# Attention and gated FFN on one Trainium2 core: the last scores of batch 3 moved to the end of group 1, and the steady pattern begun one group earlier

## The chip, the cores and the metric

The kernel runs on one core of one Trainium2 chip. The metric is the device time of one execution in microseconds. The profile's span is about 1.8 us shorter than the time of the same run. A single-core run has no second die to be compared with; all runs that are used here were counted as undisturbed ("fast"). In the profile, PE is the matmul engine (TensorE), PEld its loading of weights, ACT is ScalarE, DVE is VectorE, POOL is Pool (GpSimd), and SPq is the DMA queue of SP; L281 is line 281 of the kernel. "Issue" is time in which an engine waited for nothing that the profile shows.

## The reference

```python
# attention: 8 batches, 8 heads, 576 positions, head size 64; window of 128, ALiBi slopes
scores = scale * q @ k.T
scores = where((rel >= 0) & (rel < 128), scores - slope * abs(rel), -1e9)
attn   = exp(scores - max); attn /= attn.sum() + 1e-9
x      = (attn @ v) -> 4608 tokens x 512
# FFN: 512 -> 1536 -> 512
out = (gelu(x @ w_gate) * (x @ w_val)) @ w_out
```

## The kernel before

The FFN goes over the tokens in nine groups of 512. Group g first computes 12 blocks (gate and value), then 8 half pieces of the output. The attention of later batches (576 tokens each) is woven into it: the scores of batch g+2 stand between the output pieces of group g. Then come a batch's row sums and reciprocals (parts 0 and 1 of the tokens), the spreading of the reciprocals over the partitions, and the product with v. Group 3 needs batch 3's values.

Reciprocals are spread in one of two ways. Batches 0 to 3 use matmuls. From batch 4 on it is done by DMA: one small transfer to DRAM (`rd`) and two that read it back, broadcast (`rb`). K and q of batches 2 and up are turned by DMA transposes. All these go through one queue, that of SP, in program order.

```python
    def transposes_dma(b):                       # L156: key first, then query
        for src, dst in ((ks, kT), (qs, qT)):
            nc.sync.dma_start_transpose(out=dst[b % 2]..., in_=src[b % 2]...)
    ...
    def sums(b, s):                              # L221: 24 matmuls with ones
        ps = bank()                              # one of 8 PSUM banks, in rotation
        ...
        nc.vector.reciprocal(sumrow[b][:, lo:hi], ps[:, 0:hi - lo])          # L230

    def spread_dma(b):
        d = d_pool.tile([4, 2, S], FP32, name="rd")
        nc.sync.dma_start(out=d..., in_=sumrow[b][0:128:16, :])              # L234
        for i in (0, 1):
            nc.sync.dma_start(out=recip[b][64 * i:64 * i + 64, :, :], ...)   # L236

    def spread_pe(b, s):                         # L244: fp32 matmuls, then copies (L251)
        ...
    def values(b, s, cs):                        # L262 matmuls with v, L268 product
        ...
    def gate_val(g, f):                          # L281, two banks; gelu L285, product L286
        ...
    def out_half(g, u):                          # L297, half of an output piece; osb L302
        ...
    todo = { 0: [...],
        1: [("s2", 2), ("s", 2, 0, (0, 1)), 0, ("s", 2, 0, (2, 3)), 1, 2,
            ("s", 2, 1, (0, 1), lambda: sums(2, 0)), 3, ("s", 2, 1, (2, 3)), ("s2", 3),
            ("spread", 2, 0), ("pv", 2, 0), 4, ("sum", 2, 1), ("s", 3, 0, (0, 1)), 5, 6,
            ("spread", 2, 1), ("pv", 2, 1), ("s", 3, 0, (2, 3)), 7],
        2: [("s", 3, 1, (0, 1), lambda: sums(3, 0)), 0, ("s", 3, 1, (2, 3)), 1,
            ("spread", 3, 0), ("pv", 3, 0), ("s2", 4), ("sum", 3, 1), 2,
            ("s", 4, 0, (0, 1)), 3, ("spread", 3, 1), ("pv", 3, 1), 4, ("s", 4, 0, (2, 3)), 5,
            ("s", 4, 1, (0, 1)), 6, 7, ("s", 4, 1, (2, 3))],
    }
    def steps(g):                                # the steady pattern, b = g + 2
        ...
        return [("s2", b), ("s", b, 0, (0, 1)), 0, 1, ("s", b, 0, (2, 3)), 2, 3,
                ("s", b, 1, (0, 1)), 4, 5, ("s", b, 1, (2, 3)), 6, 7]

    for g in range(NG):
        for b in ((), (2, 3), (4,))[g] if g < 3 else ():
            transposes_dma(b)                    # batch 4: at the start of group 2
        if g + 2 < B:
            load_v(g + 2)                        # Pool's queue; waits for values(g)
        for f in range(3 if g == 0 else 0, NF):
            gate_val(g, f)
            ...
            if 3 <= g < B - 1:
                if f == 0:
                    sums(g + 1, 0)
                    sums(g + 1, 1)
                    spread_dma(g + 1)
                    if g + 2 < B:
                        transposes_dma(g + 2)
                elif f in (8, 10):
                    for s in (0, 1):
                        values(g + 1, s, (f - 8, f - 7))
        if g + 3 < B:
            load_qk(g + 3)                       # Pool's queue; waits for transposes_dma(g + 1)
        for item in steps(g): ...
```

The softmax here doesn't subtract the row's maximum and nothing guards it: scores larger than these inputs give would overflow.

Of the kernel before, what the change touches and what calls it, by code (L numbers as in the profile page):

```python
# [26 lines left out]
def kernel(  # L27
# [11 lines left out]
    B, H, S, D = q.shape  # L39
# [23 lines left out]
    def bank():  # L63
        return psum.tile([128, 512], FP32, name="ps")
# [23 lines left out]
    def load_qk(b):  # L88
        load(qs[b % 2], q, b)
        load(ks[b % 2], k, b)  # L90
# [18 lines left out]
    def load_v(b):  # L109
        load(vb[b % 2], v, b)  # L110
# [28 lines left out]
    def transpose(b, what, c, copy):  # L139
        ps = bank().bitcast(BF16)  # L140
        for j in range(5):
            nc.tensor.transpose(  # L142
                out=ps[:, 128 * j:128 * j + 128],
                in_=(qs, ks)[what][b][:, j, 128 * c:128 * c + 128], identity=ident)
        copy(out=(qT, kT)[what][b][:, :, c, :],
             in_=ps[:, 0:640].rearrange("p (j t) -> p j t", t=128))
# [7 lines left out]
    def transposes_dma(b):  # L154
        for src, dst in ((ks, kT), (qs, qT)):
            nc.sync.dma_start_transpose(  # L156
                out=dst[b % 2].rearrange("p j c t -> p (j c) t"),
                in_=src[b % 2].rearrange("p j x -> p (j x)"))
# [49 lines left out]
    def prob(b, s, c, i, j, n):  # L208
        if (s, j) == (0, 2):
            return probs2[b][:, c, i, 0:n]  # L210
        return probs[b, s, c][:, i, PCOL[s][j]:PCOL[s][j] + n]
# [3 lines left out]
    def sums(b, s):  # L215

        ps = bank()
        for j, a, e in PIECES[s]:
            for i in (0, 1):
                for c in range(4):  # L220
                    nc.tensor.matmul(  # L221
                        out=ps[32 * c:32 * c + 32, a:e],
                        lhsT=ones[:, min(j, 1), i, :], rhs=prob(b, s, c, i, j, e - a),
                        start=(i == 0 and j == 2 * s), stop=(i == 1 and j == 2 * s + 2),
                        skip_group_check=True)
        if s == 0:
            sumrow[b] = r_pool.tile([128, S], FP32, name="r")
            recip[b] = r_pool.tile([128, 4, S], FP32, name="rb")
        lo, hi = PART[s]
# [4 lines that stand above are left out]
        nc.sync.dma_start(out=d.rearrange("c i s -> (c i) s"), in_=sumrow[b][0:128:16, :])  # L234
        for i in (0, 1):
            nc.sync.dma_start(  # L236
                out=recip[b][64 * i:64 * i + 64, :, :],
                in_=d[:, i, :].unsqueeze(0).to_broadcast((64, 4, S)))
# [14 lines left out]
    def values(b, s, cs):  # L253
        lo, hi = PART[s]
        pss = []
        for c in cs:
            ps = bank()
            pss.append(ps)
            for j, a, e in PIECES[s]:
                for i in (0, 1):  # L260
                    h = 2 * c + i
                    nc.tensor.matmul(  # L262
                        out=ps[64 * i:64 * i + 64, a:e],
                        lhsT=vb[b % 2][:, j, 64 * h:64 * h + 64],
                        rhs=prob(b, s, c, i, j, e - a),
                        start=(j == 2 * s), stop=(j == 2 * s + 2), skip_group_check=True)
        for c, ps in zip(cs, pss):
            nc.vector.tensor_tensor(  # L268
                out=xT[:, c, b * S + lo:b * S + hi], in0=ps[:, 0:hi - lo],
                in1=recip[b][:, c, lo:hi], op=ALU.mult)  # L270
# [3 lines left out]
    def gate_val(g, f, lo=0, hi=512):  # L274
        if g not in hid:
            hid[g] = h_pool.tile([128, NF, 512], BF16, name="hT")
        t0 = 512 * g
        pg, pv = bank(), bank()
        for w, ps in ((wg, pg), (wv, pv)):
            for c in range(4):  # L280
                nc.tensor.matmul(  # L281
                    out=ps[:, 0:hi - lo], lhsT=w[:, c, 128 * f:128 * (f + 1)],
                    rhs=xT[:, c, t0 + lo:t0 + hi], start=(c == 0), stop=(c == 3))
        gl = g_pool.tile([128, 512], BF16, name="gelu")
        nc.scalar.activation(out=gl[:, 0:hi - lo], in_=pg[:, 0:hi - lo], func=AF.Gelu)  # L285
        nc.vector.tensor_tensor(out=hid[g][:, f, lo:hi], in0=pv[:, 0:hi - lo],  # L286
                                in1=gl[:, 0:hi - lo], op=ALU.mult)
# [3 lines left out]
    def out_half(g, u):  # L291
        t, half = u // 2, u % 2
        if half == 0:
            acc[g] = bank()
        po = acc[g]
        for f in range(6 * half, 6 * half + 6):
            nc.tensor.matmul(  # L297
                out=po, lhsT=hid[g][:, f, 128 * t:128 * (t + 1)],
                rhs=wo[:, f, :], start=(f == 0), stop=(f == NF - 1))
        if half == 1:  # L300
            osb = o_pool.tile([128, DM], FP32, name="osb")
            nc.scalar.copy(out=osb, in_=po)  # L302
            r0 = 512 * g + 128 * t
            nc.sync.dma_start(out=out[r0:r0 + 128, :], in_=osb)
# [83 lines left out]
    for t in (qs[0], ks[0]):  # L388
# [11 lines left out]
        1: [("s2", 2), ("s", 2, 0, (0, 1)), 0, ("s", 2, 0, (2, 3)), 1, 2,  # L400
            ("s", 2, 1, (0, 1), lambda: sums(2, 0)), 3, ("s", 2, 1, (2, 3)), ("s2", 3),
            ("spread", 2, 0), ("pv", 2, 0), 4, ("sum", 2, 1), ("s", 3, 0, (0, 1)), 5, 6,
            ("spread", 2, 1), ("pv", 2, 1), ("s", 3, 0, (2, 3)), 7],
        2: [("s", 3, 1, (0, 1), lambda: sums(3, 0)), 0, ("s", 3, 1, (2, 3)), 1,
            ("spread", 3, 0), ("pv", 3, 0), ("s2", 4), ("sum", 3, 1), 2,
            ("s", 4, 0, (0, 1)), 3, ("spread", 3, 1), ("pv", 3, 1), 4, ("s", 4, 0, (2, 3)), 5,
            ("s", 4, 1, (0, 1)), 6, 7, ("s", 4, 1, (2, 3))],
    }

    def steps(g):  # L410
        b = g + 2
        if g in todo:
            return todo[g]
        if b >= B:
            return range(8)
        return [("s2", b), ("s", b, 0, (0, 1)), 0, 1, ("s", b, 0, (2, 3)), 2, 3,
                ("s", b, 1, (0, 1)), 4, 5, ("s", b, 1, (2, 3)), 6, 7]
# [2 lines left out]
           "pv": lambda b, s: values(b, s, range(4))}  # L420

    for g in range(NG):
        for b in ((), (2, 3), (4,))[g] if g < 3 else ():
            transposes_dma(b)
        if g + 2 < B:
            load_v(g + 2)
        for f in range(3 if g == 0 else 0, NF):
            gate_val(g, f)
            if g == 0 and f >= 8:
                for w in (0, 1):  # L430
                    transpose(1, w, f - 8, (act, dve)[w])
            if 3 <= g < B - 1:
                if f == 0:
                    sums(g + 1, 0)
                    sums(g + 1, 1)
                    spread_dma(g + 1)
                    if g + 2 < B:
# [5 lines that stand above are left out]
            load_qk(g + 3)  # L443
        for item in steps(g):
            if isinstance(item, int):
                out_half(g, item)
            else:
                RUN[item[0]](*item[1:])
# [30 lines left out]
```

## Time and profile before

| | before |
|---|---|
| time, median of 3 runs | 367.69 us (367.64 to 367.73) |
| span of the profiled run | 365.5 us |
| PE busy | 347.8 us, 95% |
| first FFN matmul of groups 2, 3 (PE's timeline) and 4, 5 (chain of waits) | 111.78, 151.99, 190.14, 227.54 us |
| a steady group (4 and later) | 37.40 us |

Where PE did not wait, the chain starts a block 0.08 to 0.16 us later than PE's timeline does (190.14 against 189.98).

The page gives each engine's busy share. The chain of waits gives, in order of time, the work that set the end: start, length, engine and line. A long unbroken run of PE pieces means that only PE's work counts there; a piece of another engine or of a DMA means that PE stood still for it. The timelines give each engine's instructions with the idle time before them and what ended it, in brackets. The lines are in the prediction below.

### The profile page before, as it was taken

To read this page: it belongs to the slowest core of one execution; us is meant where nothing else is said; L and a number is where in the kernel's file an instruction comes from. 1 tells how busy PE (TensorE), PEld (TensorE's weight loads), DVE (VectorE), ACT (ScalarE), POOL (GpSimd) and SP (SyncE) were. 2 spreads that over 40 slices of the span, in tenths; PEclk is the share of its full clock that TensorE was granted. 3 is DMA by queue.
4 is the path that set the end of the run, shared out by engine and by line. 5 is a ranking of instruction groups with operands and counts; after the bars stand their busy time and mean duration, and the time that the engine had idled before them with its cause. 6 is when DMAs were issued, how large, how long until landed. Compare 5 with 4: busy or idle time off the path is not lost.

```text
span 365.5 us, 6601 instructions
## 1 busy us (share of the span) xinstructions
PE 347.8 (95%) x2614; PEld 171.3 (47%) x2656; DVE 188.6 (52%) x306; ACT 187.3 (51%) x339; POOL 107.9 (30%) x140
## 2 busy tenths in 40 slices
PE   3799999999999999999999999999999999999995
PEld 2455545444454445444445444444444444444442
DVE  4794448543695469475547454655564404302320
ACT  5863487434966376943783368436842223323321
POOL 8945859913519202900850040000000000000000
PEclk9779999999999999999999999999999999999999
DMA  9999999999969994999991992094205020011002
GB/s 103 136 199 178 177 163 184 174 153 200 162 116 121 136 92 81 143 103 217 127 196 50 228 97 89 33 221 53 87 32 131 0 109 7 0 60 58 0 29 88
DMA packets 151168, 41.41 MB, mean 113 GB/s; under 512 B 138816, under 2 KB 144448, under 8 KB 151136
## 3 DMA queue, kind: packets, MB, share of 16 engines
q0 software_dynamic: 112608, 18.88, 67.8%
q1 hardware_dynamic: 38528, 22.10, 27.2%
q8 instruction: 21, 0.34, 0.4%
q14 instruction: 11, 0.09, 0.1%
HBM read 42.47 MB, written 9.51 MB: 142 GB/s over the span
## 4 chain that ended last, share of the span: by engine, by line
PE 86%; ACT 5%; DVE 3%; DMA 3%; issue 1%; POOL 1%; POOLq 0%; SPq 0%; ACTq 0%; DVEq 0%
PE ps L281 50%; PE ps L297 23%; PE ps L262 4%; ACT P L170 4%; PE ps L163 4%; DMA qT<-qs 3%; PE ps L221 2%; PE ps L244 2%; DVE r L230 1%; DVE P L173 1%; DVE xT L268 1%; ACT emask L346 1%; PE ps L142 1%; POOL ks L104 0%; ACT L170 0%
## 5 line engine op out<-in xcount | busy, mean ns | idle before, releaser
L286 DVE TENSOR_TENSOR hT<-ps,gelu 128x512 bf16<-128x512 f32 (+2 forms) x111 | 74.3, 674 | 121.9 <-PE ps L281 109.3
L285 ACT ACTIVATE gelu<-ps 128x512 bf16<-128x512 f32 (+2 forms) x111 | 64.9, 585 | 119.6 <-PE ps L281 117.2
L281 PE MATMUL ps<-xT,wg 128*128 128x512 bf16 (+2 forms) x430 | 110.6, 374 | 0.8
L281 PE MATMUL ps<-xT,wv 128*128 128x512 bf16 (+2 forms) x435 | 110.4, 373 | 0.6
L297 PE MATMUL ps<-wo,hT 128*128 128x512 bf16 x413 | 97.2, 380 | 1.5 <-issue 0.6
L170 ACT ACTIVATE P<-ps 128x512 bf16<-128x512 f32 x144 | 74.4, 632 | 7.1 <-PE ps L163 7.0
L281 PEld LDWEIGHTS <-wv 128*128 128x128 bf16 x444 | 43.3, 98 | 50.3 <-issue 0.2
L281 PEld LDWEIGHTS <-wg 128*128 128x128 bf16 x444 | 41.9, 98 | 48.9 <-issue 1.1
L173 DVE TENSOR_TENSOR P<-P,emask 128x1024 bf16<-128x1024 bf16 x72 | 48.3, 685 | 31.3 <-ACT P L170 31.0
L297 PEld LDWEIGHTS <-hT 128*128 128x128 bf16 x432 | 39.8, 98 | 49.0 <-issue 4.4
L84 POOL DMA_DIRECT2D vb<-in_v_dram x40 | 33.7, 862 | 75.8 <-PE ps L262 75.0
L302 ACT COPY osb<-ps 128x512 f32<-128x512 f32 x36 | 21.7, 603 | 37.2 <-PE ps L297 32.8
L84 POOL DMA_DIRECT2D qs<-in_q_dram x35 | 29.6, 877 | 24.9 <-DMA qT<-qs 12.9
L230 DVE RECIPROCAL r<-ps 128x320 f32<-128x320 f32 (+1 forms) x16 | 30.7, 1939 | 3.1 <-PE ps L221 3.1
L84 POOL DMA_DIRECT2D ks<-in_k_dram x35 | 29.6, 887 | 6.4 <-DMA qs<-in_q_dram 3.0
L163 PE MATMUL ps<-qT,kT 64*128 64x256 bf16 (+1 forms) x384 | 24.0, 254 | 3.0 <-DVE kT L136 1.3
L268 DVE TENSOR_TENSOR xT<-ps,rb 128x320 bf16<-128x320 f32 (+1 forms) x64 | 24.7, 449 | 0.8 <-DMA rb<-rd 0.8
L163 PEld LDWEIGHTS <-kT 64*128 64x128 bf16 x384 | 13.1, 96 | 16.9 <-issue 11.6
L262 PE MATMUL ps<-P,vb 128*64 128x128 bf16 (+2 forms) x384 | 19.4, 251 | 0.1
L262 PEld LDWEIGHTS <-vb 128*64 128x64 bf16 x384 | 15.4, 113 | 7.3 <-issue 7.2
L221 PE MATMUL ps<-P,ones 128*32 128x128 bf16 (+2 forms) x384 | 11.6, 256 | 1.3 <-DVE P L173 1.3
L221 PEld LDWEIGHTS <-ones 128*32 128x32 bf16 x384 | 8.5, 101 | 5.6 <-issue 4.5
(47 smaller groups left out, 91.3 us busy)
## 6 DMA issues: line engine op xcount, KB each, us to landing
out_dram<-osb SPq DMA_DIRECT2D x36, 256.0 KB, 2.7
rb<-rd SPq DMA_DIRECT2D x8, 576.0 KB, 7.1
vb<-in_v_dram POOLq DMA_DIRECT2D x32, 128.0 KB, 4.7
qs<-in_q_dram POOLq DMA_DIRECT2D x28, 128.0 KB, 6.7
ks<-in_k_dram POOLq DMA_DIRECT2D x28, 128.0 KB, 6.4
wg<-in_moe_w_gate_dram POOLq DMA_DIRECT2D x4, 384.0 KB, 11.0
wv<-in_moe_w_val_dram POOLq DMA_DIRECT2D x4, 384.0 KB, 12.2
wo<-in_moe_w_out_dram POOLq DMA_DIRECT2D x2, 768.0 KB, 10.9
```

Of the source, the lines that this page charges most:

```text
L84: nc.gpsimd.dma_start(out=t[lo:128, j, :].rearrange("p (h d) -> p h d", h=H), in_=src[b][:, 128 * j - 64 + lo:128 * j + 64, :].rearrange(" ...
L163: nc.tensor.matmul(out=ps[:, col:col + 128 * n].rearrange("p (n t) -> p n t", n=n), lhsT=blocks(kT, b, i, c, j, 1).rearrange("p n t -> p ( ...
L170: nc.scalar.activation(out=dst, in_=src, func=AF.Exp, scale=0.125)
L173: nc.vector.tensor_tensor(out=dst, in0=dst, in1=m, op=ALU.mult)
L221: nc.tensor.matmul(out=ps[32 * c:32 * c + 32, a:e], lhsT=ones[:, min(j, 1), i, :], rhs=prob(b, s, c, i, j, e - a), start=(i == 0 and j == ...
L230: nc.vector.reciprocal(sumrow[b][:, lo:hi], ps[:, 0:hi - lo])
L262: nc.tensor.matmul(out=ps[64 * i:64 * i + 64, a:e], lhsT=vb[b % 2][:, j, 64 * h:64 * h + 64], rhs=prob(b, s, c, i, j, e - a), start=(j == ...
L268: nc.vector.tensor_tensor(out=xT[:, c, b * S + lo:b * S + hi], in0=ps[:, 0:hi - lo], in1=recip[b][:, c, lo:hi], op=ALU.mult)
L281: nc.tensor.matmul(out=ps[:, 0:hi - lo], lhsT=w[:, c, 128 * f:128 * (f + 1)], rhs=xT[:, c, t0 + lo:t0 + hi], start=(c == 0), stop=(c == 3))
L285: nc.scalar.activation(out=gl[:, 0:hi - lo], in_=pg[:, 0:hi - lo], func=AF.Gelu)
L286: nc.vector.tensor_tensor(out=hid[g][:, f, lo:hi], in0=pv[:, 0:hi - lo], in1=gl[:, 0:hi - lo], op=ALU.mult)
L297: nc.tensor.matmul(out=po, lhsT=hid[g][:, f, 128 * t:128 * (t + 1)], rhs=wo[:, f, :], start=(f == 0), stop=(f == NF - 1))
```

## The change

The intent is to have the steady pattern from group 2 on. Batch 3's last score calls move from group 2 to the end of group 1; its sums move into group 2's FFN blocks; its reciprocals are spread by DMA in place of matmuls; and batch 4's transposes follow them in SP's queue, where they used to stand at the start of group 2. In group 2 alone the sums of part two come at `f == 2`, two blocks later than in the other groups.

```diff
             ("spread", 2, 0), ("pv", 2, 0), 4, ("sum", 2, 1), ("s", 3, 0, (0, 1)), 5, 6,
-            ("spread", 2, 1), ("pv", 2, 1), ("s", 3, 0, (2, 3)), 7],
-        2: [("s", 3, 1, (0, 1), lambda: sums(3, 0)), 0, ("s", 3, 1, (2, 3)), 1,
-            ("spread", 3, 0), ("pv", 3, 0), ("s2", 4), ("sum", 3, 1), 2,
-            ("s", 4, 0, (0, 1)), 3, ("spread", 3, 1), ("pv", 3, 1), 4, ("s", 4, 0, (2, 3)), 5,
-            ("s", 4, 1, (0, 1)), 6, 7, ("s", 4, 1, (2, 3))],
+            ("spread", 2, 1), ("pv", 2, 1), ("s", 3, 0, (2, 3)), 7, ("s", 3, 1, (0, 1)),
+            ("s", 3, 1, (2, 3))],
     }
@@
-        for b in ((), (2, 3), (4,))[g] if g < 3 else ():
+        for b in ((), (2, 3))[g] if g < 2 else ():
             transposes_dma(b)
@@
-            if 3 <= g < B - 1:
+            if 2 <= g < B - 1:
                 if f == 0:
                     sums(g + 1, 0)
+                if f == (2 if g == 2 else 0):
                     sums(g + 1, 1)
                     spread_dma(g + 1)
                     if g + 2 < B:
```

## The prediction

> **What bounds the kernel now.** I read the page's first two parts, then the chain of waits, then the timelines of PE, ScalarE, VectorE and the DMA-issuing queue around the groups that the diff touches.
>
> ```profile
> PE 347.8 (95%) x2614; PEld 171.3 (47%) x2656; DVE 188.6 (52%) x306; ACT 187.3 (51%) x339; POOL 107.9 (30%) x140
> ...
> PE   3799999999999999999999999999999999999995
> ```
>
> The reader is to see that PE is busy in every slice after the start, while the next busiest engines stand at half. So the time changes only if PE gets less work, or a gap opens or closes on PE. The chain of waits (start, length, what) gives PE's clock by group, since each group of 512 tokens begins with a stretch of L281 matmuls:
>
> ```profile
> 137.17 0.75 PE ps L244 x8
> ...
> 143.26 0.66 PE ps L244 x8
> ...
> 151.51 0.56 PE ps L163 x12
> 152.07 2.08 ACT P L170 x4
> 154.18 0.70 DVE P L173
> 154.93 0.60 PE ps L221 x21
> ...
> 190.14 1.73 PE ps L281 x8
> ...
> 227.54 1.73 PE ps L281 x8
> ...
> 264.94 1.73 PE ps L281 x8
> ```
>
> Groups 4 and 5 begin at 190.14 and 227.54, group 6 at 264.94: a steady group takes 37.40 us. The timeline of PE has group 2's first FFN matmul at 111.78 and group 3's at 151.99. So group 2 takes 40.21 us and group 3 takes 38.15, both more than steady. In group 2 the two L244 pieces are the spreading of the reciprocals by matmuls. At 152 to 155 the chain leaves PE: the sums wait for the last exponentials and mask.
>
> The steady pattern has almost no slack in one place, which the DMA queue's timeline shows (start, length of the issue, what):
>
> ```profile
> 160.48 0.71 SPq L234 DMA_DIRECT2D rd<-r  x1
> 162.36 1.35 SPq L236 DMA_DIRECT2D rb<-rd  x2
> 163.94 7.12 SPq L156 DMA_TRANSPOSE kT<-ks  x1
> 171.23 3.09 SPq L156 DMA_TRANSPOSE qT<-qs  x1
> ...
> 197.15 0.62 SPq L234 DMA_DIRECT2D rd<-r  x1
> 198.96 1.27 SPq L236 DMA_DIRECT2D rb<-rd  x2
> 200.45 6.58 SPq L156 DMA_TRANSPOSE kT<-ks  x1
> 207.20 3.08 SPq L156 DMA_TRANSPOSE qT<-qs  x1
> ```
>
> In a steady group four transfers hang behind the second reciprocal, in order. The second reciprocal ends at 160.46 and at 197.12 (VectorE's timeline: 156.70 + 3.76, 193.36 + 3.76). The query transpose, whose issue-to-landing row says 4.9 us in both windows, lands at 176.1 and 212.1. That is **15.0 to 15.7 us after the second reciprocal**. The scores that need it start at 176.88 and 214.35. So the slack was 0.7 and 2.2 us.
>
> **What the Trainium skill says.** "Perfetto Trace Analysis", Optimization Strategy: look for the gaps of the engine one optimizes for and for what releases them. That is the method here; the trace agrees that PE is that engine (95% busy). "PSUM — Partial Sum Buffer", PSUM: the matmul accumulator: eight banks, and they are PE's only way out. All eight serve this kernel in rotation, so a matmul group waits for the reader of the bank eight allocations back. "ScalarE: Activation LUTs", What ACT_TABLE_LOAD costs: a load takes about 1283 ns; the trace has 1.28 us for each. "DMA: Bandwidth & Descriptors", Issuing engines are not separate DMA queues: transfers of all issuing engines interleave on the same 16 engines. The trace agrees: a query transpose lands in 4.9 us when alone, and in 9.2 us where Pool's loads run beside it (issued at 88.54, with loads from 87.99).
>
> **The change part by part.**
>
> (a) *Removed: spreading batch 3 by matmuls.* 16 fp32 matmuls, 0.75 + 0.66 = 1.41 us of PE on the path. Four ScalarE copies (about 0.42 us each) and four VectorE copies (about 0.44) go too, off the path.
>
> (b) *Moved: the two score calls of batch 3 part two, from group 2 to the end of group 1.* PE work is the same: 24 matmuls, 0.55 us per 12, so 1.1 us. Group 1 grows by it and group 2 shrinks by it.
>
> (c) *Group 2 ends in the steady way*, with two output pieces behind the last scores. Group 3 then should be a steady group: 38.15 - 37.40 = 0.75 us gained.
>
> (d) *A new gap at the end of group 1.* Eight exponentials now stand behind the osb copy of piece 7 (start 112.25). ScalarE starts one every 0.5 us (eight took 4.03 us at 133.74). They start at 112.73 and the first ends near 113.35. PE finishes the scores near 113.0; the bank of the next FFN block is the one that this first exponential reads. So FFN block 0 starts at about **113.45** in place of 111.78: 1.1 us is the moved work, 0.57 is wait.
>
> (e) *After that no bank should be late.* Exponentials end at 116.8, the table load at 118.1, gelu 0 at 118.7, its product at 119.4. PE runs block 0 (1.73), sums (0.55), blocks 1 and 2, sums of part two, and wants block 3 at 119.75; its banks are free at 118.7 and 119.4. Block 4's first bank was read by the first reciprocal, over at 119.4 + 2.1 = 121.5, just when PE gets there. Placing the second sums behind block 2 and not block 0 makes this fit: the last mask ends near 117.5 and the second sums come at 119.2.
>
> (f) *The price: the DMA chain starts late.* VectorE's order in the changed program is product 0, reciprocal, products 1 and 2, reciprocal. The second one ends at about 121.4 + 1.3 + 1.7 = **124.4**, which is 10.9 us after block 0's start; in steady groups it is 7.0 (197.12 - 190.14) to 8.5. Behind it come rd (124.4), rb (126.3), key transpose (127.8) and query transpose (134.5). With the measured 15.0 to 15.7 it lands at 139.4 to 140.1 if alone. But Pool's loads of v for batch 5 are freed by the values of batch 3, which now end near 136, so they start while it runs. I add 0.5 to 1 us, chosen between nothing and the 4.3 us of the 9.2 us case, because only the last half overlaps. So it lands at **140.6**. PE without waiting would be at the scores of batch 4 at 113.45 + 24.2 (the steady 214.35 - 190.14) = 137.65. **PE waits 3.0 us there.** Batch 4's transposes used to be issued at 113.46, with no reciprocal ahead of them.
>
> (g) *rb lands near 134 to 135*, 9.7 to 10.5 us after the reciprocal as in the groups 3 and 4, while PE runs the first values at 130.2. VectorE sits still for some 3 us; PE feels it only at the second values (134.7), through banks, by at most half a microsecond, which is inside the wait of (f).
>
> **Sum.** From group 2's first block to group 4's, before: 190.14 - 111.78 = 78.36. After: 1.67 of (d), two steady groups 74.80, and the wait W of (f): 76.47 + W. That is a gain of 1.89 - W (the 1.41 and 0.75 of (a) and (c), some 0.3 of small issue gaps, less the new 0.57). With W = 3.0 the kernel loses 1.1 us: 367.69 + 1.1 = **368.8 us**. Nothing behind group 4 changes.
>
> **The rivals.** *A pure gain*: the query transpose comes in time, W near 0, 365.8 us. For it: (a) is certain, and the 2.2 us of slack in group 4 shows that the chain can be early. Against: the second reciprocal is some 4 us later in its group, more than that slack. *A larger loss*: Pool's loads slow the query transpose to its 9.2 us; it lands at 144, W is 6, 371.8 us. For it: that happened twice in the first groups. Against: those had loads beside them from their first moment, here only in the second half. *ScalarE becomes the bound at the seam*: if gelu 0 waits for more than I think, blocks 3 and 4 lose 1 to 2 us, but the chain of (f) moves with the reciprocals too, so the total rises by about the same amount: 370. For it: the banks of block 3 and 4 are free only just in time; against: ScalarE's durations there are well known.
>
> **Range and chances.** The terms (a) to (d) are known to 0.3 us; W is 1.4 to 4.7. So 367.2 to 370.4 holds it 8 times in 10, with 368.8 as the middle. The 2% line is 7.35 us away on either side; faster by that is not in the PE work removed, and slower needs a stall twice the worst one above: 0.01, 0.97, 0.02.
>
> **What would show each step.** (a): L244 with 48 matmuls in place of 64. (d): FFN of group 2 at 113.3 to 113.6 and ScalarE's table load ending near 118.1. (e): no PE gap over 0.3 us in blocks 0 to 8 of group 2. (f): the query transpose issued near 134.5, landing near 140.6, PE idle about 3 us before the s2 scores of batch 4, released by qT. (g): VectorE waiting about 3 us for rb. (c): groups 3 and 4 each 37.40. The prediction is wrong if qT lands before 138, if blocks 3 to 6 stall, or if group 3 loses its steady length to later loads.

## The result

The changed kernel took 372.94 us (median of 6 runs, 371.24 to 375.73), the kernel before beside it 367.72 (6 runs, 367.64 to 367.99). The ratio is 1.0146, 95% interval 1.0106 to 1.0186. Ratios here are the mean time of one kernel's fast runs over the mean of the other's from the same rounds, so not quite the ratio of the medians. By the 2% rule this is "same"; in truth the kernel is slower by about 5 us, and in these rounds its runs scatter over 4.5 us where those of the kernel before scatter over 0.35. The predicted 368.8 and its range up to 370.4 were too low.

The profiled run is the fastest of the six (371.24, span 369.5); the other five have no profile. First its page, the busy times and the row of PE over 40 slices:

```profile
PE 348.0 (94%) x2599; PEld 171.4 (46%) x2640; DVE 187.1 (51%) x302; ACT 186.1 (50%) x335; POOL 108.0 (29%) x140
...
PE   3899999999999995999999999999999999999995
```

PE's busy time did not fall although 1.4 us of matmuls went (the slower clock below is part of the answer), and a slice near 140 us, which used to be full, is half empty. The chain of waits shows the place (start, length, what):

```profile
111.69 0.78 PE ps L163 x18
112.47 0.66 ACT P L170
...
113.17 1.89 PE ps L281 x8
...
134.85 7.29 DMA qT<-qs
142.14 0.14 issue
142.28 1.47 PE ps L163 x16
...
156.87 1.73 PE ps L281 x8
...
194.27 1.73 PE ps L281 x8
```

Group 2 begins at 113.17 and group 3 at 156.87, so group 2 takes 43.70 us, 6.3 more than a steady group. Group 3 takes 194.27 - 156.87 = 37.40, as hoped. So the whole loss lies in group 2. Below, "the seam" is the place in group 2 where PE passes from the FFN blocks to the scores of batch 4 and the output pieces. The chain leaves PE for the query transpose of batch 4. PE's own timeline gives the wait in front of the first scores of batch 4, and Pool's and VectorE's timelines show what else went on:

```profile
142.28 1.47 PE L163 MATMUL ps<-qT,kT 64*128 64x128 bf16 x16 [4.43 <-DMA qT<-qs]
```

```profile
135.71 4.19 POOL L84 DMA_DIRECT2D vb<-in_v_dram  x5 [14.85 <-PE ps L262]
142.68 4.19 POOL L84 DMA_DIRECT2D qs<-in_q_dram  x5 [2.79 <-DMA qT<-qs]
```

```profile
134.59 1.55 DVE L268 TENSOR_TENSOR xT<-ps,rb 128x320 bf16<-128x320 f32 x4 [3.54 <-DMA rb<-rd]
```

SP's queue then reads as below. Compare the steady groups in the prediction: the order is the same, but it starts 10.9 us into the group and not 7.

```profile
124.08 0.71 SPq L234 DMA_DIRECT2D rd<-r  x1
125.94 1.32 SPq L236 DMA_DIRECT2D rb<-rd  x2
127.49 7.19 SPq L156 DMA_TRANSPOSE kT<-ks  x1
134.85 3.96 SPq L156 DMA_TRANSPOSE qT<-qs  x1
```

One more view, the busy time of the engines in stretches of 3 us (stretch, length, busy of PE, PEld, DVE, ACT and POOL with counts, granted PE clock, DMA share, GB/s), shows something that the prediction had not looked for:

```profile
137.00:140.00 3.00, 0.85 (x4) 0.20 (x2) 2.40 (x6) 1.88 (x2) 2.90 (x4) 1.00 1.36 259
140.00:143.00 3.00, 0.72 (x12) 0.72 (x14) 0.00 (x0) 0.11 (x1) 0.32 (x1) 0.79 2.33 148
143.00:146.00 3.00, 2.78 (x15) 1.20 (x13) 1.41 (x3) 2.94 (x6) 3.00 (x5) 0.64 1.32 84
```

The granted clock is 1.00 before the wait and falls around its end: 0.79 and 0.64 in two stretches of 3 us. If the clock is either full or half, that is (0.21 + 0.36) x 3 / 0.5 = 3.4 us at half speed. The first scores take 1.47 us where steady groups have 0.77, and from their start to group 3 it takes 14.59 us (142.28 to 156.87) where the steady pattern has 13.19 (176.95 to 190.14): 1.4 us more. This is what the Trainium skill describes in "TensorE: Matmul & The Clock Gate", The HAM clock gate: the clock drops to half after an idle window of about 3.4 us and comes back after a busy one. I had not applied it. The kept profiles agree: behind each wait of PE at the seam of 4.15 us or more (this one, e0, e3, e4, e7 below) the clock stood at half for 3.4 to 6.8 us, and behind none of those of 1.16 to 2.76 us (e1, e2, e10, e11).

### The profile page after: what moved, and what is told of

Read it like the earlier page. It is cut to its first block, busy times and chain, and to the rows that moved or that the text cites. A ratio compares the mean times of both kernels' runs of the same rounds, so it can differ in the third digit from the quotient of the medians.

```text
span 369.5 us, 6563 instructions
## 1 busy us (share of the span) xinstructions
PE 348.0 (94%) x2599; PEld 171.4 (46%) x2640; DVE 187.1 (51%) x302; ACT 186.1 (50%) x335; POOL 108.0 (29%) x140
## 4 chain that ended last, share of the span: by engine, by line
PE 83%; ACT 7%; DVE 4%; DMA 2%; issue 2%; POOL 1%; SPq 0%; POOLq 0%; DVEq 0%; ACTq 0%
PE ps L281 50%; PE ps L297 23%; ACT P L170 4%; PE ps L163 4%; PE ps L262 4%; PE ps L221 2%; DMA qT<-qs 2%; DVE P L173 2%; DVE xT L268 1%; DVE r L230 1%; PE ps L244 1%; ACT L170 1%; ACT emask L346 1%; PE ps L142 1%; POOL ks L104 0%
## 5 line engine op out<-in xcount | busy, mean ns | idle before, releaser
L163 PE MATMUL ps<-qT,kT 64*128 64x256 bf16 (+1 forms) x384 | 24.9, 263 | 7.4 <-DMA qT<-qs 4.8
```

Source lines behind the costliest of these rows:

```text
L163: nc.tensor.matmul(out=ps[:, col:col + 128 * n].rearrange("p (n t) -> p n t", n=n), lhsT=blocks(kT, b, i, c, j, 1).rearrange("p n t -> p ( ...
```

## The experiments

**The theory after the first look.** (1) Batch 4's query transpose comes late because it hangs behind the second reciprocal. (2) Pool's loads of v beside it stretch its landing from 4.9 to 7.3 us. (3) PE's wait exceeds the clock's idle window, so the clock falls to half. **The rivals.** The late softmax chain of batch 4 on ScalarE and VectorE sets the end of group 2; the scores moved to the end of group 1 cost in themselves; the transpose is slow there for another reason; the clock dip costs nothing or has another cause.

Twelve kernels were run, all correct against the reference. All edits are against the changed kernel. They ran in three sets on three chips (e1 to e4; e0, e5, e8, e9; e6, e7, e10, e11), each with the kernel before beside it, whose medians were 367.72, 367.47 and 367.76. Across sets, compare the ratios.

| run | edit | us, median (lowest to highest), runs | ratio to before (95%) |
|---|---|---|---|
| e0_again | none | 372.84 (372.72 to 373.5), 4 | 1.0148 (1.0131 to 1.0165) |
| e1_pieces_first | two output pieces ahead of batch 4's scores | 368.53 (367.4 to 371.19), 20 | 1.0030 (1.0012 to 1.0047) |
| e2_v_after_qk | loads of v behind those of q, k | 368.64 (367.49 to 370.92), 20 | 1.0029 (1.0014 to 1.0044) |
| e3_key_first | key transpose at the start of group 2 | 371.9 (370.31 to 372.67), 4 | 1.0109 (1.0082 to 1.0136) |
| e4_both_first | both transposes at the start | 375.07 (374.04 to 375.61), 4 | 1.0199 (1.0175 to 1.0222) |
| e5_warm | idle PE kept busy | 370.51 (370.28 to 371.59), 5 | 1.0089 (1.0070 to 1.0107) |
| e6_sums_at_0 | both sums behind block 0 | 367.84 (366.92 to 369.09), 12 | 0.9999 (0.9986 to 1.0011) |
| e7_sums_at_1 | sums of part two behind block 1 | 371.82 (371.47 to 372.45), 4 | 1.0109 (1.0091 to 1.0128) |
| e8_pieces_and_v | e1 and e2 | 366.52 (365.57 to 369.62), 14 | 0.9988 (0.9967 to 1.0008) |
| e9_scores_only | half of the change | 367.91 (367.39 to 369.3), 13 | 1.0007 (0.9995 to 1.0020) |
| e10_piece0_sums1_v | one piece ahead, sums behind block 1, e2 | 366.7 (365.97 to 367.35), 11 | 0.9965 (0.9953 to 0.9976) |
| e11_piece0_sums1 | one piece ahead, sums behind block 1 | 370.83 (367.35 to 372.49), 8 | 1.0069 (1.0035 to 1.0103) |

### Fill the wait: e1_pieces_first

```diff
+        if g == 2:
+            return [0, 1, ("s2", b), ("s", b, 0, (0, 1)), 2, 3, ("s", b, 0, (2, 3)), 4, 5,
+                    ("s", b, 1, (0, 1)), 6, ("s", b, 1, (2, 3)), 7]
```

> Edit: in group 2 the output pieces 0 and 1 stand ahead of the s2 scores of batch 4, so PE has 2.7 us of other work while the query transpose is on its way. Theory (PE waits for the query transpose that starts late, and the clock falls to half because of the wait): the transpose lands when it did, near 142.1; PE's wait shrinks from 4.4 to about 1.7 us, no half-clock window at the seam, time 367.5 to 369. Rival (the loss is not the wait itself but the late start of batch 4's whole softmax chain, so ScalarE and VectorE set the end of group 2): the time stays at 371 to 373.

The transpose landed at 142.32, as before, and PE's wait fell from 4.43 to 1.29 us. The time fell by 4.4 us. The late softmax chain is thereby no bound: it starts as late as in the changed kernel. The 20 runs show the clock's part. The 7 with a mean granted clock of 0.995 or 0.989 took 369.33 to 371.19 us; the 11 with 0.998 or more took 367.40 to 368.56. One half-clock window of 3.4 us lowers the mean over 366 us by about 0.005, so the slower ones most likely had one. This is a correlation only, since in those runs the transpose may have landed later too. The other two runs, 0.985 at 367.87 us and 0.981 at 370.37, show that a low mean alone proves nothing about the seam. Two kept profiles have a mean of 0.985, that of the kernel before and that of e2: there the clock stands at half for some 10 us between 12 and 24 us, at the start of the program, and is full at the seam. That early stretch costs little: with it these runs took 367.30 and 367.63 us, among the fastest of their kernels. A mean of 0.981 fits the early stretch and one window more.

### Take the loads away from the transpose: e2_v_after_qk

```diff
-        if g + 2 < B:
+        if g + 2 < B and g != 3:
             load_v(g + 2)
@@
             load_qk(g + 3)
+        if g == 3:
+            load_v(g + 2)
```

> Edit: Pool issues batch 5's loads of v behind those of q and k for batch 6, which wait for the query transpose, so no load runs beside that transpose. Theory (contention stretched its landing from 4.9 to 7.3 us): it lands 4.9 to 5.2 us after its issue near 134.8, at about 139.8; PE waits 2 us, no half-clock window, time 367.8 to 369.2. Rival (the transpose is slow there for another reason): it lands at 7 us or more and the time stays at 371 to 373.

Batch 6's loads of q and k wait for the query transpose of batch 4, whose source they overwrite. What is put behind them in Pool's queue cannot run beside that transpose. The chain of waits:

```profile
134.56 5.31 DMA qT<-qs
139.87 0.14 issue
140.01 0.83 PE ps L163 x16
```

The transpose was issued as late as in the changed kernel (134.56) but landed 5.3 us after its issue and not 7.3 to 8.0, as in all six profiles that have the loads beside it (after, e0, e1, e5, e7, e11). The wait was 1.90 us, the first scores took 0.83 us, full clock. So the loads of v did stretch it, by 2 to 2.7 us. How they do it shows in the profile's count of DMA packets by queue, taken in short stretches of time (q1 is SP's queue, q0 Pool's). In the changed kernel 2944 packets of q1 moved from 137 to 139.9 us, nearly all before the first packets of the loads, which came only at about 139.7 although Pool had begun to issue them at 135.71. But 32 packets of q1 were left, and these moved between 140 and 142 us among 2287 of q0; the transpose landed at 142.14. SP had issued nothing else, so I take them for the end of the transpose. In e0 the same number, 32, came between 142.0 and 143.5. So in these profiles the loads hold up the last packets, not the bulk. Of the 20 runs 7 still had a mean clock of 0.994 or 0.995, and those took 369.49 to 370.92 us; their waits are not in a profile.

### Issue the transposes early: e3_key_first and e4_both_first

```diff
 # e3: key transpose at the start of group 2, query transpose behind the spreading
+        if g == 2:
+            transposes_dma(4, (0,))
@@
-                        transposes_dma(g + 2)
+                        transposes_dma(g + 2, (1,) if g == 2 else (0, 1))
 # e4: both at the start of group 2, as in the kernel before
-        for b in ((), (2, 3))[g] if g < 2 else ():
+        for b in ((), (2, 3), (4,))[g] if g < 3 else ():
@@
-                    if g + 2 < B:
+                    if g + 2 < B and g != 2:
                         transposes_dma(g + 2)
```

> Edit: the key transpose of batch 4 is issued at the start of group 2, as in the kernel before; only the query transpose stays behind the two reciprocals and their spreading. Theory (the chain behind the second reciprocal is too long by one transpose): query transpose issued near 127.5 and landed by 133 to 135, no wait of PE for it, groups 2 and 3 both near 37.4 us, time 365.5 to 366.5, below the kernel before. Rival (the early key transpose meets Pool's loads, delays rd and rb, and VectorE's wait for rb then holds PE through the banks): PE waits 1 to 3 us at the second values of group 2, time 367 to 369.

> Edit: both transposes of batch 4 at the start of group 2, exactly as in the kernel before, the spreading of batch 3 behind them. Theory: no wait for the query transpose, but it is issued until about 127 beside Pool's loads, so rd and rb follow 2 to 3 us later than in the changed kernel; VectorE waits for rb until about 137 and PE waits about 2 us at the second values of group 2; time 367 to 368.5. Rival (rb's time does not matter, only the query transpose does): 365.5 to 366.5, the same as with the key transpose alone moved.

Both were slow: 371.9 and 375.07 us, the second slower than the changed kernel. My theory for e3 fell, and its named rival, a wait for rb, was right in kind but too small (1 to 3 us). For e4 the wait for rb was the theory, at 2 us, and that was too small as well. SP's queue in e3:

```profile
113.38 5.10 SPq L156 DMA_TRANSPOSE kT<-ks  x1
124.25 0.71 SPq L234 DMA_DIRECT2D rd<-r  x1
129.27 1.31 SPq L236 DMA_DIRECT2D rb<-rd  x2
130.74 8.35 SPq L156 DMA_TRANSPOSE qT<-qs  x1
```

The early key transpose runs beside Pool's loads of batch 5, and those end later: the last of them was issued at 124.73 and not by 121. Then the rd transfer of 18 KB, issued at the same time as in the changed kernel (124.25 against 124.08), let rb follow only after 5.0 us, not 1.9. PE's timeline in e3 and then in e4:

```profile
139.55 1.55 PE L262 MATMUL ps<-P,vb 128*64 128x192 bf16 x18 [4.15 <-DVE xT L268]
```

```profile
142.11 1.54 PE L262 MATMUL ps<-P,vb 128*64 128x192 bf16 x18 [5.86 <-DVE xT L268]
```

VectorE waits for rb (7.8 us in e3, 9.5 in e4), its banks stay full, and PE waits 4.2 and 5.9 us at the second values of batch 3. The clock then stands at half for about 6.8 us in both profiles (0.80, 0.50 and 0.56 in three stretches of 3 us in e3), twice as long as in the changed kernel, which is part of their times. In e9 below the transposes have their old place too, with no spreading by DMA behind them, and it does no harm. In these runs one of the two chains waited, whichever came first in the queue.

### What the half clock costs: e5_warm beside e0_again

```diff
+    def warm(n):
+        ps = bank()
+        for _ in range(n):
+            nc.tensor.matmul(out=ps, lhsT=wo[:, 0, 0:128], rhs=wo[:, 1, :], start=True, stop=True)
@@
+        if g == 2:
+            return [("warm", 20), ("s2", b), ...the steady pattern...]
```

> The changed kernel once more, for the spread of its runs beside the others on this chip. Theory (PE idles over 4 us for the query transpose; how long, and how many half-clock windows of 3.4 us follow, varies from run to run): median 371.5 to 373.5, runs from about 371 to 376. Rival (the first six runs were scattered by chance): all runs within 1 us.

> Edit: 20 matmuls of 128x512 whose result nobody reads (4.3 us of PE) stand in group 2 where PE waits for the query transpose. Their output is thrown away; the kernel's result is unchanged. Theory (the idle stretch lets the clock fall to half for one or two windows, which costs 1 to 2 us after the wait): the transpose lands when it did, the s2 scores start when they did (near 142.2), no half-clock window at the seam, s2 takes 0.8 and not 1.5 us, median 1 to 2 us below the changed kernel on the same chip, and a narrower spread. Rival (the clock dip is not caused by idling, or costs nothing): the median is that of the changed kernel or up to 0.3 us above.

The 20 matmuls produce nothing that is used; they take one more bank in the rotation. The chain of waits of e0_again, then that of e5_warm:

```profile
143.63 1.46 PE ps L163 x16
145.10 3.49 PE ps L297 x12
148.59 0.54 PE ps L163 x8
```

```profile
142.68 0.84 PE ps L163 x16
143.52 2.70 PE ps L297 x12
146.21 0.54 PE ps L163 x8
```

The same 28 matmuls take 4.95 us in the one and 3.54 in the other, a difference of 1.4 us. In e5_warm the granted clock is 1.00 throughout; in e0_again it is 0.54 and 0.89 in the stretches 143 to 146 and 146 to 149, which is 0.46 x 3 / 0.5 + 0.11 x 3 / 0.5 = 3.4 us at half again. The medians on the same chip differ by 2.3 us. 1.4 of that is the clock at the seam; of the rest, 0.65 us is in how long after group 2's start the transpose landed in these two profiles (29.60 against 28.95), which I take for scatter and cannot prove. e0_again's four runs lay within 0.8 us, so the scatter of the first six was not reproduced on this chip, and that part of the expectation missed.

### The start of the chain: e7_sums_at_1 and e6_sums_at_0

```diff
-                if f == (2 if g == 2 else 0):
+                if f == (1 if g == 2 else 0):      # e7
+                if f == 0:                         # e6
```

> Edit: the sums of part two of batch 3 stand behind FFN block 1 and not 2. Theory (the wait is set by when the DMA chain behind the second reciprocal starts): that reciprocal ends 0.6 us earlier, before product 2; no new gap on PE, since the last mask ends at 117.3, when PE gets there; the query transpose is issued and lands about 0.6 us earlier; PE waits about 3.8 us; time 0.6 to 1.5 us below the changed kernel: 371.3 to 372.3 where it has 372.84. Rival (the landing is set by the loads beside it, not by the chain's start): no change, 372.5 to 373.5.

> Edit: both sums of batch 3 behind FFN block 0, as in the steady groups. Theory: PE has to wait about 1.6 us for the last mask (ends 117.3) in block 0, but the second reciprocal ends 1.2 us earlier and the query transpose lands 1.2 us or more earlier, so PE's wait there falls below 2 us and the clock stays full: 368.5 to 370.5, faster than the changed kernel although it has one more wait. Rival (the gap behind block 0 is a pure addition): 373.5 to 374.5.

With the sums behind block 1, rd was issued 0.6 us earlier in its group (10.3 us after the first block against 10.9), and the median was 371.82, as expected. The profile bears it out less well: PE waited 4.22 us where 3.8 was expected, since the transpose took 7.8 us to land. With both sums behind block 0 the kernel took 367.84 us. PE's timeline of e6:

```profile
117.42 0.22 PE L221 MATMUL ps<-P,ones 128*32 128x128 bf16 x1 [0.63 <-DVE P L173]
118.40 0.60 PE L221 MATMUL ps<-P,ones 128*32 128x128 bf16 x21 [0.76 <-DVE P L173]
```

There PE waits 1.4 us for the last masks of batch 3, the wait that the changed kernel had avoided by moving the sums to `f == 2`. It wins about 5 us for it, against e0 and the first six runs. The reciprocals come 1.2 us earlier in the group, and the gap makes everything else on PE 1.4 us later, also the values of batch 3 and with them Pool's loads of v (issued at 138.29, 3.8 us behind the query transpose and not 0.9). At the scores of batch 4 (140.54) PE waited for nothing. My expectation had 368.5 as its lower end, so the gain was larger than I thought: I had counted the earlier chain but not the later loads.

### Half of the change: e9_scores_only

```diff
 # batch 4's transposes at the start of group 2 and no spread_dma/values in its FFN, as before;
 # batch 3's reciprocals spread by matmuls among group 2's output pieces
+        if g == 2:
+            return [("s2", 4), ("spread", 3, 0), ("pv", 3, 0), 0, ("s", 4, 0, (0, 1)), 1, 2,
+                    ("spread", 3, 1), ("pv", 3, 1), ("s", 4, 0, (2, 3)), 3, 4,
+                    ("s", 4, 1, (0, 1)), 5, ("s", 4, 1, (2, 3)), 6, 7]
```

> Half of the change: the last scores of batch 3 at the end of group 1 and its sums in group 2's FFN as in the changed kernel, but batch 3's reciprocals still spread by matmuls in group 2's second half, and both transposes of batch 4 at its start, as in the kernel before. Theory (the moved scores cost only the half microsecond of bank wait at the seam, and the whole loss comes from the DMA chain of spreading and transposing): no wait over 0.6 us on PE, group 2 takes 37.4 + 1.4 us, group 3 takes 37.4, time 366.7 to 367.5. Rival (moving the scores to the end of group 1 itself costs): 368.5 or more, with waits in the first blocks of group 2.

At 367.91 us (ratio 1.0007, interval across 1) it is as fast as the kernel before, so moving the scores to the end of group 1 is not what costs. It is 0.4 us above my expected range: in its profile the chain of waits leaves PE behind the first spreading matmuls for two exponentials (137.04 to 138.13), and the 24 matmuls with v beside them take 1.65 us where those in a steady group take 1.13. My order of pieces made this half microsecond, and I had not foreseen it.

### Versions that could win: e8_pieces_and_v, e11_piece0_sums1, e10_piece0_sums1_v

e8 is e1 and e2 together. e11 moves one output piece ahead of batch 4's scores and the sums of part two behind block 1; e10 adds e2's edit to e11.

```diff
 # e10 and e11
+        if g == 2:
+            return [0, ("s2", b), ("s", b, 0, (0, 1)), 1, 2, ("s", b, 0, (2, 3)), 3, 4,
+                    ("s", b, 1, (0, 1)), 5, ("s", b, 1, (2, 3)), 6, 7]
-                if f == (2 if g == 2 else 0):
+                if f == (1 if g == 2 else 0):
```

> Edit: both working edits together, pieces 0 and 1 ahead of the s2 scores of batch 4 and the loads of v behind those of q and k. Theory: query transpose lands near 139.9, PE is busy until about 140.5, so it waits for nothing at the seam; group 2 takes 37.4 to 37.6 us from its first block; 1.5 to 2 us below the kernel before, 365.7 to 366.4. Rival (another wait, for rb or for ScalarE at the end of group 2, takes its place): 367 or more.

> Edit: one output piece ahead of the s2 scores of batch 4 (1.35 us of PE work in the wait) and the sums of part two behind block 1; loads as in the changed kernel. Theory: query transpose lands near 141.5 still beside the loads of v, PE ready at 139.1, waits about 2.4 us, full clock: 368 to 369.3.

> Edit: the run with one piece and the sums behind block 1, and the loads of v behind those of q and k. Theory: query transpose lands near 139.3, PE ready at 139.1, wait under 0.5 us; groups 2 and 3 near 37.6 each; 1 to 1.8 us below the kernel before: 365.7 to 366.5. Rival (group 3's transposes then meet the later loads and PE waits there, as 2 us of group 3 did with both pieces ahead): 367 to 368.

e8 has the lowest median, 366.52, just above the expected 366.4, but some runs up to 369.6, and its interval reaches across 1. In its profiled run (367.46) group 2 took 37.89 us and group 3 took 39.39: there group 3's own query transpose landed late (6.3 us after its issue, at 177.09) and PE waited 1.93 us for it. The rival named for e8 was a wait in group 2; this one had not been foreseen, and became the rival of e10. e11 missed its expectation: 370.83, with runs from 367.35 to 372.49. Its profiled run had a wait of 2.76 us (expected: 2.4) and full clock; five of the eight had a mean clock of 0.991 to 0.995 and took over 370 us. PE's timeline of e10 at the seam:

```profile
140.86 0.84 PE L163 MATMUL ps<-qT,kT 64*128 64x128 bf16 x16 [1.16 <-DMA qT<-qs]
```

e10 is e11 without the contention, and gains 4.1 us on it on the same chip. Its ratio is 0.9965 with an interval of 0.9953 to 0.9976: **1.1 us faster than the kernel before by the medians, and faster than the changed kernel by about 6**. Its median is 0.2 us above the expected range. Its wait was 1.16 us, more than the half microsecond expected, as the transpose needed 5.9 us and not 4.9 even with no load of v beside it; why is not shown. Its group 3 took 37.4 us, so the rival did not come.

## Why the prediction was wrong, by its own steps

- **(a)** Right: 48 of the L244 matmuls are left of 64.
- **(b), (d)** Right: group 2 began at 113.17 (predicted 113.45), with the wait for one exponential at 112.47 in the chain.
- **(c)** Right: groups 3 and 4 took 37.40 and 37.39 us. The gain was a little smaller than 0.75, as that figure sets a start from PE's timeline (151.99) against one from the chain (190.14); by the timeline alone group 3 took 37.99 us before, which makes 0.6.
- **(e)** Right: no gap in blocks 0 to 8 of group 2; the second reciprocal ended near 124.05 (predicted 124.4).
- **(g)** Right: rb held VectorE for 3.54 us (predicted 3), and PE did not wait at the second values.
- **(f)** Here it failed. The mechanism was right, the wait for the query transpose; the issue time was right (134.85 against 134.5). The size of W was not. *First mis-sized term*: "I add 0.5 to 1 us, chosen between nothing and the 4.3 us of the 9.2 us case, because only the last half overlaps." The transpose took 7.3 us to land in the first profile and 8.0 in e0_again, against the 4.9 us of a free one; e2 puts 2 to 2.7 us of it on the loads of v. The reason given for a small term failed: the loads' packets did overlap only with the end of the transfer, but its last 32 packets moved among theirs and landed some 2 us after the bulk. *A missing term*: the clock. The sum took PE's work behind the wait at its steady length. It was 1.4 us longer, as e5_warm shows by removing only the idling. With both, the profiled run has a wait of 4.9 us against the unstalled 137.4 (113.17 + 24.2; 142.28 is when the scores started; PE stood idle for 4.43 of it) and 1.4 us of clock: W was 6.3 us and not 3.0. The formula of the prediction then gives 1.89 - 6.3 = -4.4 us. The spans differ by 4.0 us (369.5 against 365.5); 0.25 us had been gained before the change begins, as the last output piece of group 1 started at 110.45 and not 110.70.
- **The rival "a larger loss"** named 371.8 us by a landing at 144. Its mechanism, the loads beside the transpose, was the right one. That the time came near its number is luck: it was made up of a landing at 142.1 and the clock.
- **The rival "ScalarE becomes the bound at the seam"** (of groups 1 and 2) did not come: PE has no wait in blocks 3 and 4.
- **The range** ended at W = 4.7 because I varied only the landing. The two terms are not independent: a wait that grows past the clock's idle window jumps by another microsecond or more. A range should have had that step in it.

What stays open: how much of the 4.5 us of scatter in the first six runs is the landing and how much the clock. The mean granted clocks of those runs (0.995 for the two fastest, 0.991 for two in the middle, 0.985 for the slowest, but 0.982 for one of 372.53) could be one to three half-clock windows at the seam; but the early stretch found in other profiles lowers a mean to 0.985 by itself, so 0.985 and 0.982 say nothing certain, and only one run in six has a profile.

## What to carry to other kernels

When a chain of transfers is moved behind a later event, ask which loads become free to start at that same time and run beside it: moving the last link by 4 us cost 2 more by contention and 1.4 by the clock. A short wait put in early on purpose can be cheaper than a long one later: the 1.4 us gap of e6 saved 5 us. And where PE has to wait, put independent matmuls there, above all when the wait comes near the clock's idle window.

## What the Trainium skill lacked or had wrong

- "DMA: Bandwidth & Descriptors", Issuing engines are not separate DMA queues: says that transfers interleave, but not by how much a DMA transpose suffers. Here the query transpose landed in 4.9 to 5.7 us in groups 3 and 4 of the changed kernel, in 5.3 (e2) and 5.9 (e10) in group 2 with no loads of v beside it, and in 7.3 to 8.0 with 0.6 MB of small-packet loads beside its end. In the two profiles looked at (after, e0) the last 32 packets moved among those of the loads, some 2 us behind the bulk.
- The same page, Latency and other measured facts, has no figure for a small transfer behind a filled queue. An 18 KB transfer let its successor start after 1.9 us in the changed kernel, and after 5.0 (e3) and 5.9 us (e4) when early transposes had delayed Pool's loads into its time.
- "ScalarE: Activation LUTs", What ACT_TABLE_LOAD costs: gives about 1283 ns for the load and 1380 ns of drain, 2.66 us for a switch. The load is confirmed (1.28 us); the drain is not seen here: the load started at 116.57, right behind the last exponential (112.46 + 4.09 = 116.55), and the first gelu at 117.86, so the switch took 1.3 us in all.
